# A planned attention and two feed-forward layers on one core: offsets on the planner's due times, one load for q and k, the last output in three pieces

## The chip, the core and the metric

The kernel runs on one core of a Trainium2 chip. The metric is the device time of one launch in microseconds (us). The engines are TensorE (PE in the profile, its weight loads PEld), VectorE (DVE), ScalarE (ACT), GpSimd (POOL) and SyncE (SP), which here issues every DMA.

## What is computed

Causal attention with a decay bias, 4 batches of 8 heads, 576 positions of 64 values; its output is seen as 2304 tokens of 512 values and goes through two feed-forward layers. Cut to what matters:

```python
scores = scale * np.matmul(q, k.transpose(0, 1, 3, 2))
bias = -(cum[:, :, :, None] - cum[:, :, None, :])
scores = np.where(causal, -1000000000.0, scores + np.minimum(bias, 0.0))
attn = np.exp(scores - scores.max(-1)); attn = attn / (attn.sum(-1) + 1e-09)
x = np.matmul(attn, v)                      # then as (2304, 512)
h = x @ w_in
x = (h * np.cos(h)) @ w_out                 # 512 -> 2048 -> 512
xn = x / np.sqrt(np.mean(x * x) + 1e-06) * rms_g
g = xn @ w_gate
out = (g / (1 + np.exp(-g)) * (xn @ w_val)) @ w_out2   # 512 -> 1536 -> 512
```

## The kernel before, in words

The Python program does not issue instructions as it goes. Each step is recorded with `plan.op(...)` (line 139): the engines that could run it with an estimated cost, the tiles it reads and writes, and a due time `plan.now + prio`. `Plan.order()` (line 156) then plays the whole program through a list scheduler with these estimated costs: an engine that is free takes, of the steps whose inputs are ready, the one with the smallest due time. The chip gets the result, one fixed list for each engine. On the chip an engine runs its list strictly in order and waits at each entry for its inputs, so a step that is late there holds up everything behind it on that engine. Two constants bend the choice: `HOLD` is added to the due time of an activation that needs another table than the one loaded, `KEEP_MODE` to a TensorE step of another array mode. Where a step has several engines, the one with the smallest estimated finish is taken, its own cost multiplied by `WEIGH` (line 133).

**Attention** goes over 16 pairs of heads. A pair loads q and k (lines 467 to 470, one transfer each into rings `qr` and `kr` of two buffers), its bias rows `ce` and `cp` (lines 473 to 476) and v. POOL writes the causal mask into the bias (line 491, line 484). TensorE makes scores (line 551; line 575 for the ragged last 64 positions), DVE adds the bias and takes the row minimum in one custom instruction (line 558, line 578; called "the bias step" below; its tile of minima is `mn`), ACT takes the exponential in place (line 586), TensorE transposes it (line 601), ACT or DVE copies the transpose from PSUM to `Pa` or `Pb` (line 336 on ACT, line 339 on DVE), TensorE multiplies by v (line 635), ACT or DVE copies to `xu`. Row sums are inverted (lines 513 and 515), go through DRAM (`rn_d`) and come back broadcast; DVE scales `xu` (line 347, the helper for all two-input steps) and the result is stored to `x_d`.

**Weights of the first layer** arrive as 64-bit integers' halves and are rebuilt by `value` (line 422): one step on POOL (line 430) or, as the other choice, on ACT (line 431), one on POOL (line 434), two on DVE (lines 435 and 437), then a split in two parts. 32 such chunks are done beside the attention.

**First layer (FF1).** Blocks of 256 or 512 tokens; each of 48 ticks does `gemm1` (line 734), cosine on ACT and DVE (`Sin` on line 852), a split, and `gemm2` (line 740). Its due times start at `T_FF1`, so its first ticks fill TensorE during the attention: tick k is due at `T_FF1 + k * P_FF1`, `gemm2` 1.6 `P_FF1` later, the weights' loads `LEAD_I` or `LEAD_O` earlier. Attention steps are due along `P_ATT` per pair. Transposed scores, scores and `gemm1` share the eight PSUM banks.

**Second layer (FF2)** multiplies on line 990 and line 1131 with seven products in place of eight block products. The last part (line 1131) goes over 9 units of 7 products `m`; a unit has two output tiles `o1` and `o2` of 128 rows by 512, stored whole at `m == 6` (lines 1154 to 1156).

The lines that say it shortest:

```python
o.alts, o.prio, o.table, o.dma = alts, self.now + prio, table, dma
t = max(ready, free[e] + ahead) + c * self.WEIGH[e]
_, _, o = min((o.prio + (self.HOLD if o.table and o.table != table else 0.0) + ..., o.seq, o)
              for o in avail[e] if o.ready <= t)
```

Of the kernel before, what the change touches and what calls it, by code (L numbers as in the profile page):

```python
# [44 lines left out]
P_ATT, P_FF1, P_SET, P_OUT = 6000.0, 8093.98, 7350.0, 2145.0  # L45
T_FF1 = 45000.0
# [235 lines left out]
def attention_moe_moe(ctx, tc, q2, k2, vp, s, w_in, w_out, w_gate, w_val, w_out2, rms_g, out):  # L282
# [120 lines left out]
    qr_r, kr_r = ring("qr", 2, [128, 640], F32, "att"), ring("kr", 2, [128, S], F32, "att")  # L403
# [18 lines left out]
    def value(src, after=()):  # L422
# [31 lines left out]
    class Run:  # L454


        def __init__(self, bp, parts):
            self.bp, self.b, self.p = bp, bp // NP, bp % NP
            self.qs = slice(0 if "a" in parts else 256, 640 if "b" in parts else 256)
            self.ks, self.vc = (S, 5) if "b" in parts else (256, 2)  # L460
            self.parts = {c: Part(self, c) for c in parts}
            self.col = {k: i for i, k in enumerate([(0, t) for t in range(4)] + ["p"] + [(1, t) for t in range(4)])}

        def load(self):
            bp, qn, ks = self.bp, self.qs.stop - self.qs.start, self.ks
            q, k = self.q, self.k = qr_r.new(), kr_r.new()
            load(lambda: q()[:, :qn], lambda: bass.AP(q2.tensor, q2.offset + bp * 128 * 640 + self.qs.start, [[640, 128], [1, qn]]), 512 * qn, [], [q], prio=0.0 if bp else -4.9e5)
            load(lambda: k()[:, :ks], lambda: bass.AP(k2.tensor, k2.offset + bp * 128 * S, [[S, 128], [1, ks]]), 512 * ks, [], [k], prio=0.0 if bp else -4.8e5)
# [10 lines left out]
        def masks(self, ts):  # L479
            c, cp = self.ce, self.cp  # L480
            for t in ts:
                if t == "p":
                    for e in range(2):
                        plan.op(on("POOL", 416, lambda e=e: pool.affine_select(
                            out=cp()[64 * e:64 * e + 64, 512:S], in_=cp()[64 * e:64 * e + 64, 512:S], pattern=[[-1, 64]], base=0, channel_multiplier=1,
                            compare_op=ALU.is_ge, fill=-8.0 * BIG)), [], [(cp, e)])
                else:
                    for e in range(2):
# [4 lines left out]
                            compare_op=ALU.is_ge, fill=-8.0 * BIG)), r, w)  # L493

        def load_v(self):
# [4 lines left out]
                 lambda: bass.AP(vp.tensor, vp.offset + self.bp * 128 * 640, [[640, 128], [1, 640]]), 327680, [], [vr])  # L500
# [9 lines left out]
        def factors(self):  # L510
# [3 lines left out]
                out=rs(), in0=rs(), scalar1=1e-9, scalar2=float(2.0 * np.pi), op0=ALU.add, op1=ALU.mult)), [], [rs])  # L514
            plan.op(on("DVE", 204, lambda: dve.reciprocal(out=rs(), in_=rs())), [], [rs])
            plan.op(on("PE", 109, lambda: pe.transpose(tr()[:9, :128], rs(), ident)), [rs], [tr], rows=0.1)
            copy(lambda: rt()[:9, :], lambda: tr()[:9, :128], 128, [tr], [rt], psum=True)
# [497 lines left out]
    n = 0  # L1015
# [194 lines left out]
```

## Time and profile before

| | us |
|---|---|
| median of 3 runs | 1005.22 |
| lowest and highest run | 1005.15, 1007.66 |
| the profiled execution | 1007.61 |
| its span, first to last instruction | 1005.6 |
| TensorE busy in that span | 986.7 |
| mean granted clock of TensorE | 0.996 of full speed |

The span is what the rows of the trace add up to; the profiled execution's own time stands 2.0 us above it and 2.4 us above the median. TensorE's busy time counts modelled ends of pipelined matmuls, so short waits between two matmuls can be hidden in it. A row of the view by stretches gives the stretch, its length, then busy us of PE, PEld, DVE, ACT and POOL with the number of instructions, the granted clock, the share of the DMA engines and GB/s. In rows of the timeline the bracket says how long the engine had stood idle and who released it.

### The profile page before, as it was taken

The page shows a single profiled execution, that of the slowest core. Times are in us where ns is not written, and L with a number is a line of the kernel's source. Part 1 is how long each engine was busy: PE and PEld are TensorE (multiplying, and loading weights), DVE is VectorE, ACT ScalarE, POOL GpSimd, SP SyncE. Part 2 cuts the span into 40 slices and gives each one's busy share as a digit, 9 for nine tenths or more (in the row PEclk, how much of TensorE's full clock was granted, in tenths as well). Part 3 has the DMA queues.
Part 4 walks back from the last instruction along what each step waited for, and adds up shares of the span by engine and source line. Part 5 has one row for each costly group of instructions (what it writes and reads, how often), then busy time and mean ns, then how long its engine had stood idle before and what let it go on. Part 6 is the DMA issues. An engine that isn't in the chain of part 4 may idle for free.

```text
span 1005.6 us, 17817 instructions
## 1 busy us (share of the span) xinstructions
PE 986.7 (98%) x5950; PEld 853.0 (85%) x5950; DVE 738.7 (73%) x1691; ACT 560.3 (56%) x1213; POOL 125.6 (12%) x252
## 2 busy tenths in 40 slices
PE   8899999999999999999999999999999999999998
PEld 5556776668988887877878999999999999999998
DVE  4688899885357799779766988865665678986661
ACT  6799998886456566557544765212211225575540
POOL 2444354520001101110110000000000000000000
PEclk9899999999999999999999999999999999999999
DMA  8899988966846774566644464827465477997761
GB/s 259 270 306 315 314 308 277 300 225 183 281 179 235 273 265 183 217 213 221 241 158 156 139 208 143 254 88 235 138 215 179 139 215 224 305 336 220 217 191 43
DMA packets 144237, 222.95 MB, mean 222 GB/s; under 512 B 13985, under 2 KB 98097, under 8 KB 144145
## 3 DMA queue, kind: packets, MB, share of 16 engines
q1 hardware_dynamic: 144144, 221.82, 67.5%
q8 instruction: 47, 0.77, 0.3%
q14 instruction: 46, 0.37, 0.1%
HBM read 146.71 MB, written 75.06 MB: 221 GB/s over the span
## 4 chain that ended last, share of the span: by engine, by line
PE 75%; DVE 11%; DMA 6%; issue 4%; ACT 2%; POOL 2%; SPq 0%; POOLq 0%; DVEq 0%; ACTq 0%
PE bank L990 25%; PE bank L734 15%; PE bank L740 14%; PE bank L1131 13%; DVE wk L347 3%; PE bank L635 2%; PE bank L601 2%; PE bank L551 2%; DVE wk L435 1%; DVE wg L347 1%; DVE wk L437 1%; DMA rn_d<-rt 1%; POOL wk L434 1%; DVE e L558 1%; DMA wk<-in_w_gate_dram 1%
## 5 line engine op out<-in xcount | busy, mean ns | idle before, releaser
L734 PE MATMUL bank<-xa,wi 128*128 128x256 f32 (+1 forms) x1152 | 216.7, 340 | 0.5 <-ACT Pb L336 0.5
L347 DVE TENSOR_TENSOR wk<-wk,bank 128x384 f32<-128x384 f32 (+2 forms) x237 | 130.6, 556 | 115.0 <-PE bank L990 39.2
L734 PEld LDWEIGHTS bank<-xa,wi 128*128 128x128 f32 x1152 | 180.1, 188 | 29.6 <-issue 1.9
L740 PE MATMUL bank<-wr,wg 128*128 128x512 f32 x672 | 165.8, 396 | 0.8 <-ACT wg L336 0.7
L740 PEld LDWEIGHTS bank<-wr,wg 128*128 128x128 f32 x672 | 125.1, 188 | 30.8 <-ACT wg L336 2.8
L990 PE MATMUL bank<-wr,wg 128*128 128x384 f32 x504 | 116.2, 338 | 0.0
L990 PE MATMUL bank<-wi,wg 128*128 128x384 f32 x504 | 115.4, 337 | 0.2 <-DVE t L347 0.2
L336 ACT ACTIVATE wg<-wk 128x512 fp32r<-128x512 f32 (+1 forms) x138 | 78.2, 579 | 48.5 <-DVE wk L347 33.8
L347 DVE TENSOR_TENSOR wg<-wk,wg 128x512 fp32r<-128x512 f32 (+1 forms) x148 | 89.4, 625 | 20.4 <-ACT wg L336 19.5
L434 POOL TENSOR_SCALAR wk<-wk 128x512 f32<-128x512 f32 x68 | 54.8, 809 | 327.8 <-ACT wk L431 307.8
L990 PEld LDWEIGHTS bank<-wr,wg 128*128 128x128 f32 x504 | 91.2, 188 | 0.0
L990 PEld LDWEIGHTS bank<-wi,wg 128*128 128x128 f32 x504 | 89.3, 188 | 1.2 <-DVE t L347 0.6
L850 ACT ACTIVATE wk<-bank,quarter 128x512 int32<-128x512 f32 x72 | 49.3, 684 | 55.1 <-PE bank L734 54.7
L586 ACT ACTIVATE e<-e,mn 128x128 f32<-128x128 f32 (+3 forms) x128 | 70.7, 555 | 9.4 <-DVE mn L558 9.0
L336 ACT ACTIVATE wr<-wr 128x384 fp32r<-128x384 f32 x108 | 55.8, 524 | 34.8 <-DMA wr<-g_S 15.0
L336 ACT ACTIVATE wk<-bank 128x512 f32<-128x512 f32 (+2 forms) x66 | 33.8, 531 | 73.8 <-PE bank L990 52.5
L852 ACT ACTIVATE wk<-wk,half_pi 128x512 f32<-128x512 f32 x72 | 52.1, 723 | 38.9 <-DVE wk L347 38.5
L1131 PE MATMUL bank<-wi,wr 128*128 128x256 f32 x585 | 73.7, 281 | 0.0
L347 DVE TENSOR_TENSOR wk<-bank,wk 128x512 f32<-128x512 f32 (+1 forms) x82 | 54.9, 669 | 23.4 <-ACT wk L852 23.3
L1131 PEld LDWEIGHTS bank<-wi,wr 128*128 128x128 f32 x585 | 71.2, 188 | 0.0
L435 DVE SCALAR_TENSOR_TENSOR wk<-wk 128x512 int32<-128x512 int32 x68 | 49.2, 725 | 21.2 <-POOL wk L434 21.2
L347 DVE TENSOR_TENSOR wr<-wr 128x384 fp32r<-128x384 f32 x108 | 56.6, 552 | 10.3 <-ACT wr L336 9.7
(126 smaller groups left out, 1547.5 us busy)
## 6 DMA issues: line engine op xcount, KB each, us to landing
wk<-in_w_out_dram SPq DMA_DIRECT2D x28, 512.0 KB, 4.7
wr<-g_S SPq DMA_DIRECT2D x54, 192.0 KB, 2.6
w_g<-wg SPq DMA_DIRECT2D x18, 512.0 KB, 3.4
w_v<-wg SPq DMA_DIRECT2D x18, 512.0 KB, 2.9
wr<-g SPq DMA_DIRECT2D x48, 192.0 KB, 3.5
g_S<-wk SPq DMA_DIRECT2D x45, 192.0 KB, 2.4
wk<-in_w_in_dram SPq DMA_DIRECT2D x16, 512.0 KB, 6.1
wo_d<-wg SPq DMA_DIRECT2D x16, 512.0 KB, 6.0
```

The costliest lines, as they stand in the source:

```text
L336: alts.append(("ACT", (act_p if psum else act_s)(n), lambda: act.activation(o(), i(), AF.Copy, scale=scale)))
L347: return plan.op(on("DVE", dve1(n), lambda: dve.tensor_tensor(out=o(), in0=a(), in1=b(), op=op)), r, w, **kw)
L434: plan.op(on("POOL", 660, lambda: pool.tensor_scalar(out=top().bitcast(F32), in0=top().bitcast(F32), scalar1=0.0, scalar2=1.0, op0=ALU.mul ...
L435: plan.op(on("DVE", 640, lambda: dve.scalar_tensor_tensor(out=top(), in0=low(), scalar=29, in1=top(), op0=ALU.logical_shift_right, op1=ALU ...
L551: pe.matmul(Sp[e]()[:, o:o + w], run.q()[hd, q0:q0 + 128], run.k()[hd, :w], start=True, stop=True)
L586: plan.op(on("ACT", act_s(w) + 187, lambda E=E, o=o, w=w, i=i, c=c: act.activation(E()[:, o:o + w], E()[:, o:o + w], AF.Exp, scale=-1.0, b ...
L734: pe.matmul(h, w[:, a, 128 * k:128 * k + 128], x[k // 2][:, k % 2, c, :blk], start=(n == 0), stop=(n == 11))
L740: pe.matmul(acc[t], g[a][:, 128 * t:128 * t + 128], w[:, c, :], start=(first and (a, c) == (0, 0)), stop=(last and (a, c) == (1, 0)))
L850: plan.op(on("ACT", act_p(512) + 93, lambda u=u, h=h: act.activation(u().bitcast(I32), h(), AF.Identity, bias=quarter)), [h], [u])
L852: plan.op(on("ACT", 628, lambda u=u: act.activation(u(), u(), AF.Sin, scale=-TWO_PI, bias=half_pi)), [], [u], table="sin")
L990: pe.matmul(bank_()[:, :HALF2], G[i]()[:, u, o + 128 * k:o + 128 * k + 128], xs[k]()[:, c, :], start=(first and n == 0), stop=(n == 5), sk ...
L1131: pe.matmul(bk_()[:, col:col + 256], gs[p // 3]()[:, u, 128 * (p % 3):128 * (p % 3) + 128], w3[p][i]()[:, c, o:o + 256], start=(n == 0), s ...
```

## The change

Three things. First, the planner's steps get an offset by kind, added to the due time (in ns, negative is earlier), and some constants change. Second, the host lays q and k side by side, 640 + 576 columns for each of a pair's 128 rows, and one transfer of 608 KB into one ring takes the place of two of 320 and 288 KB. Third, the last unit's output is stored in three pieces: the right half of `o2` after `m == 4`, `o1` after `m == 5`, the left half of `o2` after `m == 6`. The diff, cut to its core:

```diff
-LEAD_I, LEAD_O, LEAD_E = 14000.0, 10000.0, 0.0
+LEAD_I, LEAD_O, LEAD_E = 14000.0, 9847.0, 0.0
-KEEP_MODE = 1000.0
-DMA_EACH, DMA_RATE, DMA_LATE = 5.0, 21.6, 1700.0
+KEEP_MODE = 1306.0
+DMA_EACH, DMA_RATE, DMA_LATE = 5.0, 20.06, 1700.0
...
-P_ATT, P_FF1, P_SET, P_OUT = 6000.0, 8093.98, 7350.0, 2145.0
-T_FF1 = 45000.0
+P_ATT, P_FF1, P_SET, P_OUT = 6095.0, 8093.98, 7350.0, 2145.0
+T_FF1 = 47510.0
+O_LOAD, O_BIAS, O_V, O_MASK, O_SCORE, O_TTR, O_RAGGED = -1340.0, 2596.0, -218.0, -654.0, -1417.0, -2054.0, 310.0
+O_EXP, O_TR, O_P, O_PV, O_X, O_FACTOR, O_STORE = 2888.0, 96.0, -1290.0, -462.0, -4526.0, 114.0, 20.0
+O_VALUE, O_GEMM1, O_GEMM2, O_SIN, O_X1 = -1454.0, -2758.0, 2525.0, 916.0, 1195.0
...
-    WEIGH = {"PE": 1.0, "ACT": 1.0, "DVE": 2.0, "POOL": 1.0, "SP": 1.0}
-    SWITCH, HOLD = 1283.0, 30000.0
+    WEIGH = {"PE": 1.0, "ACT": 1.0, "DVE": 2.00, "POOL": 0.30, "SP": 1.0}
+    SWITCH, HOLD = 1283.0, 27846.0
...
-    qr_r, kr_r = ring("qr", 2, [128, 640], F32, "att"), ring("kr", 2, [128, S], F32, "att")
+    qk_r = ring("qk", 2, [128, 640 + S], F32, "att")
...
+            load(qk_t, lambda: qk[bp], 512 * (640 + S), [], [qk_t], run=4 * (640 + S), prio=O_LOAD if bp else -4.9e5)
...
-            for o, r0 in ((o1, 0), (o2, HALF2)) if m == 6 else ():
-                r0 += 2 * HALF2 * b + 128 * s3
-                load(lambda r0=r0: out[r0:r0 + 128, :], o, 1 << 18, [o], [])
+            r1 = 2 * HALF2 * b + 128 * s3
+            if unit < 3 * NB2 - 1:
+                parts = [(o1, 0, 0, 512), (o2, HALF2, 0, 512)] if m == 6 else []
+            else:
+                parts = {4: [(o2, HALF2, 256, 512)], 5: [(o1, 0, 0, 512)], 6: [(o2, HALF2, 0, 256)]}.get(m, [])
+            for o, r0, c0, c1 in parts:
+                load(lambda r0=r0 + r1, c0=c0, c1=c1: out[r0:r0 + 128, c0:c1], lambda o=o, c0=c0, c1=c1: o()[:, c0:c1], 512 * (c1 - c0),
+                     [o if c1 - c0 == 512 else (o, c0 // 256)], [], run=4 * (c1 - c0))
```

The offsets go to these steps: `O_LOAD` q and k, `O_BIAS` the loads of `ce` and `cp`, `O_V` v, `O_MASK` the masks, `O_SCORE` and `O_RAGGED` the scores, `O_TTR` the bias step, `O_EXP` the exponentials, `O_TR` the transposes, `O_P` the copies to `Pa` and `Pb`, `O_PV` the product with v, `O_X` its copy, `O_FACTOR` and `O_STORE` the row sums and the store, `O_VALUE` the four steps of `value`, `O_GEMM1`, `O_GEMM2`, `O_SIN` and `O_X1` FF1's parts. FF1's whole clock moves by `T_FF1`, 2510 ns later. No instruction of an engine is added or removed but for the DMAs named, and the split of line 430 against line 431.

## Rows read from the trace of the kernel before

**Rows 1.** The page's first part: busy time, share and instructions of each engine.

```profile
PE 986.7 (98%) x5950; PEld 853.0 (85%) x5950; DVE 738.7 (73%) x1691; ACT 560.3 (56%) x1213; POOL 125.6 (12%) x252
```

**Rows 2.** Stretches: length, then PE, PEld, DVE, ACT, POOL, clock, DMA, GB/s.

```profile
0.00:95.00 95.00, 86.60 (x591) 54.61 (x593) 68.65 (x238) 78.28 (x235) 37.53 (x109) 0.96 0.91 285
95.00:235.00 140.00, 134.84 (x938) 96.02 (x935) 119.71 (x317) 127.39 (x311) 58.69 (x108) 1.00 0.82 275
235.00:597.00 362.00, 361.17 (x1761) 300.36 (x1760) 273.86 (x563) 212.51 (x378) 29.34 (x36) 1.00 0.61 210
...
1002.30:1005.60 3.30, 0.00 (x0) 0.00 (x0) 0.40 (x1) 0.00 (x0) 0.00 (x0) 0.92 0.21 79
```

**Rows 3.** TensorE's waits up to 235 us: us in total, times, longest.

```profile
PE bank L601 <- ACT e L586: 4.0, 2, 3.2
PE bank L601 <- ACT Pb L336: 2.1, 3, 1.4
...
PE bank L575 <- ACT Pb L336: 1.3, 2, 1.0
PE bank L551 <- DVE mn L578: 1.2, 1, 1.2
PE bank L601 <- DVE mn L558: 1.1, 3, 0.6
PE bank L551 <- DVE mn L558: 0.6, 3, 0.2
PE bank L734 <- ACT Pb L336: 0.5, 1, 0.5
...
PE bank L575 <- ACT Pa L336: 0.3, 1, 0.3
```

**Rows 4.** The timeline between 33 and 41 us: start, us, engine, line, step.

```profile
33.91 1.78 PE L551 MATMUL bank<-kr,qr 64*128 64x128 f32 x12
...
36.51 0.54 POOL L491 TENSOR_SCALAR_AFFINE_SELECT ce<-ce 128x128 f32<-128x128 f32 x2 [2.97 <-DMA ce<-ce_d]
37.02 0.64 POOL L434 TENSOR_SCALAR wk<-wk 128x512 f32<-128x512 f32 x1
37.69 0.69 DVE L435 SCALAR_TENSOR_TENSOR wk<-wk 128x512 int32<-128x512 int32 x1 [3.61 <-POOL wk L434]
38.30 0.42 DVE L558 CUSTOM_DVE_ANT_0 e<-bank,ce 128x256 f32<-128x256 f32 x1
...
40.29 0.90 PE L601 MATMUL bank<-ident,e 128*128 128x128 f32 x3 [3.25 <-ACT e L586]
```

**Rows 5.** The stretch of the low clock, columns as in the view above.

```profile
39.10:46.00 6.90, 5.71 (x17) 3.02 (x19) 5.35 (x21) 5.57 (x21) 1.80 (x7) 0.51 0.94 286
```

**Rows 6.** Groups of ACT and of POOL up to 240 us: busy us, mean ns.

```profile
L430 POOL TENSOR_SCALAR wk<-wk 128x512 f32<-128x512 f32 x16 | 13.1, 818 | 20.2 <-DVE wg L347 13.1 <-DVE wi L347 6.2 <-issue 0.8
...
L431 ACT ACTIVATE wk<-wk 128x512 f32<-128x512 f32 x16 | 10.7, 677 | 2.5 <-DMA wk<-in_w_in_dram 1.4 <-DVE wg L347 1.0
```

**Rows 7.** SP's issues between 27 and 33 us.

```profile
27.33 0.53 SPq L351 DMA_DIRECT2D qr<-in_q_dram  x1
27.90 0.43 SPq L351 DMA_DIRECT2D kr<-in_k_dram  x1
28.44 1.03 SPq L351 DMA_DIRECT2D ce<-ce_d  x1
```

**Rows 8.** DMA issues by size: KB each, median us from issue to landing.

```profile
w_o<-wk SPq DMA_DIRECT2D x6, 256.0 KB, 2.0
...
w_o<-wk SPq DMA_DIRECT2D x6, 128.0 KB, 1.7
```

**Rows 9.** Line 430's instructions: ns min/median/max, first and last start.

```profile
L430 POOL TENSOR_SCALAR wk<-wk x16: 651/678/1165, 32.5 to 207.5; 128x512 f32<-128x512 f32 x16
```

**Rows 10.** Line 435's instructions, columns as for line 430.

```profile
L435 DVE SCALAR_TENSOR_TENSOR wk<-wk x68: 635/686/1127, 24.3 to 555.5; 128x512 int32<-128x512 int32 x68
```

**Rows 11.** The timeline of TensorE where its first FF1 matmul stands.

```profile
97.81 2.40 PE L734 MATMUL bank<-xa,wi 128*128 128x256 f32 x18 [0.48 <-ACT Pb L336]
```

More of the change, by code (lines that the diff above doesn't have):

```diff
@@ L464, in load @@
         def load(self):
[L465 to L468, printed above, removed]
+            bp, qk_t = self.bp, qk_r.new()
+            self.qk = qk_t
+            self.q, self.k = (lambda: qk_t()[:, :640]), (lambda: qk_t()[:, 640:])
+            load(qk_t, lambda: qk[bp], 512 * (640 + S), [], [qk_t], run=4 * (640 + S), prio=O_LOAD if bp else -4.9e5)
             c, cp = self.ce, self.cp = ce_r.new(), cp_r.new()
@@ L472, in load @@
                 load(lambda: c().rearrange("p e w -> p (e w)"), lambda: ce_d()[2 * bp:2 * bp + 2, :].rearrange("a b -> (a b)").partition_broadcast(128),
-                     1 << 19, [ce_d], [(c, (t, e)) for t in range(4) for e in range(2)])
+                     1 << 19, [ce_d], [(c, (t, e)) for t in range(4) for e in range(2)], prio=O_BIAS)
                 for e in range(2):
-                    load(lambda e=e: cp()[64 * e:64 * e + 64, :], lambda e=e: c_d()[2 * bp + e, :].partition_broadcast(64), 256 * S, [c_d], [(cp, e)], run=2304)
+                    load(lambda e=e: cp()[64 * e:64 * e + 64, :], lambda e=e: c_d()[2 * bp + e, :].partition_broadcast(64), 256 * S, [c_d], [(cp, e)], run=2304, prio=O_BIAS)
             else:
@@ L513, in factors @@
             plan.op(on("DVE", 130, lambda: dve.tensor_scalar(
[L514 to L517, printed above, removed]
-            load(lambda: dst().rearrange("a (b c) -> (a b) c", c=128), lambda: rt()[:9, :], 4608, [rt], [dst], run=512)
+                out=rs(), in0=rs(), scalar1=1e-9, scalar2=float(2.0 * np.pi), op0=ALU.add, op1=ALU.mult)), [], [rs], prio=O_FACTOR)
+            plan.op(on("DVE", 204, lambda: dve.reciprocal(out=rs(), in_=rs())), [], [rs], prio=O_FACTOR)
+            plan.op(on("PE", 109, lambda: pe.transpose(tr()[:9, :128], rs(), ident)), [rs], [tr], rows=0.1, prio=O_FACTOR)
+            copy(lambda: rt()[:9, :], lambda: tr()[:9, :128], 128, [tr], [rt], psum=True, prio=O_FACTOR)
+            load(lambda: dst().rearrange("a (b c) -> (a b) c", c=128), lambda: rt()[:9, :], 4608, [rt], [dst], run=512, prio=O_FACTOR)
             rb = self.rb = rb_r.new()
@@ L551, in qk @@
                         pe.matmul(Sp[e]()[:, o:o + w], run.q()[hd, q0:q0 + 128], run.k()[hd, :w], start=True, stop=True)
-            plan.op(on("PE", 110 + sum(1.668 * w for _, w in at.values()), qk), [run.q, run.k], Sp, mode=1)
+            plan.op(on("PE", 110 + sum(1.668 * w for _, w in at.values()), qk), [run.qk], Sp, mode=1, prio=O_SCORE)
             for t in reversed(ts):
@@ L601, in go @@
                     pe.transpose(tr()[:m, 128 * j:128 * j + 128], E[0]()[:, E[2] + c:E[2] + c + m], ident)
-            plan.op(on("PE", 109 * len(srcs), go), [(E[0], E[1]) for E in Es], [tr], rows=0.5)
+            plan.op(on("PE", 109 * len(srcs), go), [(E[0], E[1]) for E in Es], [tr], rows=0.5, prio=O_TR)
             cols = lambda n: tr()[:, :n].rearrange("p (c i) -> p c i", i=128)
             def out(o, src, n, P=P):
-                copy(o, src, n, [tr], [P], psum=True)
+                copy(o, src, n, [tr], [P], psum=True, prio=O_P)
             if i == 0:
@@ L644, in store @@
                 rb = self.run.rb
-                two(xu, xu, rb, S, [rb], [xu], op=ALU.mult)
-                load(lambda: xd()[:, p, :], xu, 512 * S, [xu], [(xd, p)])
+                two(xu, xu, rb, S, [rb], [xu], op=ALU.mult, prio=O_STORE)
+                load(lambda: xd()[:, p, :], xu, 512 * S, [xu], [(xd, p)], prio=O_STORE)
         def units(self):
@@ L851, in attention_moe_moe @@
             two(u, lambda u=u: u().bitcast(I32), h, 512, [h], [u], psum=True)
-            plan.op(on("ACT", 628, lambda u=u: act.activation(u(), u(), AF.Sin, scale=-TWO_PI, bias=half_pi)), [], [u], table="sin")
+            plan.op(on("ACT", 628, lambda u=u: act.activation(u(), u(), AF.Sin, scale=-TWO_PI, bias=half_pi)), [], [u], table="sin", prio=O_SIN)
             two(u, h, u, 512, [h], [u], op=ALU.mult, psum=True)
```

50 lines of the change are left out of this document (24 added, 26 removed).

## The prediction

> **What bounds the kernel now.** I read the page's busy line first [rows 1]. TensorE is busy for 986.7 of 1005.6 us, so all that any order can win by filling its idle time is 18.9 us, plus what waits hide inside "busy". The change takes no matmul away. The view by stretches says where the idle time lies [rows 2]: 8.4 us before 95 us (95 - 86.60), 5.2 us from 95 to 235 us (140 - 134.84), 0.8 us in the 362 us after that, and 3.3 us behind the last matmul. The last 770 us are a solid block of matmuls; only the attention stage and the tail can give anything. In the attention stage ACT is busy for 127.39 of 140 us and the DMA engines for 0.82 to 0.91 of the time [rows 2], so TensorE there stops for others. The table of its waits says for whom [rows 3]: for exponentials 4.0 us, for copies of the transposes to `Pb` and `Pa` 4.2 us (2.1 + 1.3 + 0.5 + 0.3), for the bias step 2.9 us (1.2 + 1.1 + 0.6).
>
> One wait stands out, of 3.25 us [rows 4]. The scores of line 551 end at 35.69 us, and the bias step of 256 columns on them stands at 38.30. DVE idled 3.61 us in between: its list has a weight step (line 435) ahead, which waits for POOL's weight step (line 434), and POOL's list has a mask ahead of that, which waits 2.97 us for the next pair's bias tile, landed at 36.51. So a late tile of the next pair stops this pair through two lists that are run in order; the exponential follows the bias step, and TensorE resumes at 40.29. Behind that stop the granted clock is 0.51 for 6.9 us [rows 5]: the lower of the two levels, 1.2 GHz. The mean of 0.96 before 95 us [rows 2] is this one dip (6.9 x 0.49 / 95 = 0.036); the rest is at 2.4.
>
> About 0.3% (3.0 us) is what a measurement of this kernel can tell from no change: "same" means 1002.2 to 1008.2.
>
> **The sum.** It is made against the profiled execution's own 1007.61 us, which is 2.4 us above the median.
>
> *Bias step ahead of weight work.* `O_TTR` moves it 2054 ns earlier; the weight steps move 2510 - 1454 = 1056 ns later with FF1's clock. That is 3.1 us of preference, so the step at 37.69 should leave its place ahead of line 558: 38.30 - 35.69 = 2.6 us [rows 4]. What is late next is the bias tile itself: it still lands at 36.51, and the next pair's first bias step needs it; I give 1.0 us back for that. Then the clock: the dip's 5.71 busy us [rows 5] would take half at full clock, so 2.85 us. The other waits of rows 3 are at most 1.4 us, and the clock stayed up behind them; a stop of about 1 us is nearer to those than to 3.25, so I count the dip as gone. Term -4.4; ends 0 and -6.1 (the whole 3.25 and the dip). Of the 2.9 us of other waits for the bias step [rows 3] I take a third, -1.0; ends 0 and -2.9.
>
> *Copies ahead of exponentials, work off ACT.* `O_P` (-1290) and `O_EXP` (+2888) put a copy 4.2 us ahead of an exponential that was due with it. POOL's weight of 0.30 turns its estimate for the first step of `value` from 700 into 210 ns against ACT's 575, so most of the 16 steps that ACT still does move: up to 16 x 0.677 = 10.7 us off ACT [rows 6], the engine with 9% idle. Half of the 4.2 us of waits for copies goes: -2.1; ends 0 and -4.2. The price is on the other side: the exponentials' own waits (4.0 us, of them 3.2 in the stop above [rows 3, 4]) can return elsewhere. +1.0; ends 0 and +4.0, those waits doubled.
>
> *q and k in one transfer.* SP's issues of a pair, 0.53 and 0.43 us [rows 7], become one, and the bias load queued behind them goes out some 0.5 us earlier. The same bytes go through the same engines, so the landing of k does not move, and the score, which needs both, waits as before. What hides it: q and k of the pair go out at 27.33 us, and its first score is in the matmuls from 33.91 us on [rows 4, 7], 6.6 us later. Term 0; ends -0.5 (the bias tile 0.5 us earlier in the stop) and +0.5, a late score once.
>
> *Bias loads later.* `O_BIAS` is +2596, but the weights' loads move by 2510 to 2663 too, so only q, k and v gain on `ce`, and q and k were ahead of it already [rows 7]. SP's list is in order: behind a late `ce` stand the weights' load and the store of `xu`, and POOL's mask waits for it. +0.7; ends 0 and +2.6, the whole offset once.
>
> *FF1's `gemm2` later.* With T_FF1 `gemm2` is due 5.0 us later and `gemm1` 0.2 earlier, so it has more slack for its weights, at most the 0.8 us idle after 235 us [rows 2]. -0.4; ends 0.8 either way.
>
> *The tail.* After the last matmul come one DVE step, a store and the end, 3.3 us [rows 2]. The last store shrinks from 256 to 128 KB; transfers of these sizes land in 2.0 and 1.7 us [rows 8]. -0.3; ends 0 and -0.6. The two earlier pieces are issued while matmuls run; if they landed late they would still end before the last.
>
> `HOLD` falls by 2.2 us of 30 while the exponentials move 2.9 and `Sin` 3.4 us (2510 + 916) later, so tables change about as often; one change more would lie in the 12.6 us that ACT idles between 95 and 235 us (140 - 127.39) [rows 2] and, if that cover is gone, in the waits for copies already counted. `KEEP_MODE` and the rest (`O_X`, `O_PV`, masks) change order within the same waits: 0, with the ends above.
>
> Sum: -4.4 - 1.0 - 2.1 + 1.0 + 0 + 0.7 - 0.4 - 0.3 = -6.5. That is 1001.1 for the profiled execution, and 1005.22 - 6.5 = **998.7 us** for the median. With all ends good it is -15.1 (990.1), with all bad +7.9 (1013.1).
>
> **The rivals.**
>
> *All waits go.* The planner weighs all steps together, and PEld's idle inside "busy" may shrink as well. Then the good ends of the first terms hold: -6.1 - 2.9 - 4.2, with the last three as above -13.2, so 992.0. For: the stops are few and each has a named cause. Against: the DMA engines at 0.91 before 95 us [rows 2] set when bias tiles land. 10%.
>
> *The waits move.* The chip's times are not the planner's, and each list is run in order, so a stop that is taken out comes back at the next late tile. Only 2.6 - 1.0 us of the stop and the tail's 0.3 remain, and the dip stays: 1003.3. The offsets then do not do what they say. For: ACT at 91% of 95 to 235 us and DVE at 86% [rows 2] leave little to rearrange. 17%.
>
> *POOL and DVE block each other.* The step on line 430 takes 651 ns at best and 818 on average, 1165 at worst [rows 6, 9]; line 435 on DVE runs from 635 to 1127 [rows 10]. If each moved step costs DVE a worst case, that is 16 x 0.49 = 7.9 us on an engine with 20.3 us idle between 95 and 235 us [rows 2]; half of it reaches TensorE, 4.0, so 1002.7. Against: line 434 waits elsewhere on its inputs, and the median of both lines is near the minimum. 8%. By the Trainium skill (SBUF — State Buffer, Who interferes with whom), a DVE instruction with two SBUF inputs contends with a GpSimd instruction that reads SBUF, and the later one is blocked fully; the spread of the rows named agrees with that, and by that rule alone the sum would be -2.5.
>
> *Slower: the bias tile of an early pair lands later.* The place is POOL's wait of 2.97 us for `ce` [rows 4]. Up to 97.81 us there is no FF1 matmul to fill in [rows 11], and the DMA engines are 0.91 busy. If `O_BIAS` lets v or a weights' load pass, a stop grows by 2.6 us and keeps its dip of 2.85: 5.4 us a pair. One such pair only eats the other gains; from two on it decides: +10.9, less 2.8 from the other terms (-1.0 - 2.1 + 1.0 - 0.4 - 0.3), gives 1013.3. Against: `ce` waits for its buffer of two pairs before, so its issue follows that release and hardly the due time. 10%.
>
> **How the numbers follow.** The forecast has 55% and lies between 995 and 1002.2. With the first rival that makes 0.65 for faster, the second and third 0.25 for the same, the last 0.10 for slower. The range is 993.0 to 1005.5: it holds the forecast and both rivals near 1003 with some room for the bad ends, and leaves out the slower rival and the far half of the first.
>
> **What would show it.** Right: no weight step that waits for POOL ahead of line 558; no dip of the clock between 30 and 50 us, mean clock 1.00 before 95 us; TensorE's idle time before 235 us at 8 to 10 us in place of 13.6; line 430 more often than 16 times up to 240 us and ACT under 85% busy between 95 and 235 us; one `qk` issue a pair; the last store landing 0.3 us sooner. Wrong: two dips, POOL's waits for `ce` longer than 3 us, or idle time after 235 us that was not there. The forecast fails as a whole if TensorE's waits for ACT and DVE stay at 11 us under other names.

## The result, and the profile after

| | before | after |
|---|---|---|
| median, us | 1005.18 (1000.93 to 1007.66, 4 runs) | 989.91 (989.80 to 990.68, 4 runs) |
| ratio, 95% interval | | 0.9854 [0.982, 0.9888] |
| profiled execution, its span, us | 1007.61, 1005.6 | 990.68, 988.8 |

The change takes 15.3 us off (1005.18 - 989.91), more than twice the 6.5 forecast, and lands 3.1 us below the range. Line numbers of the new kernel are higher: by one from the scores to the exponentials (552, 559, 587, 602, 735), by three in the helpers and in `value` (339, 350, 433, 434, 437, 438).

The busy line of the page of the kernel after answers to [rows 1]:

```profile
PE 979.8 (99%) x5950; PEld 853.2 (86%) x5950; DVE 733.4 (74%) x1671; ACT 548.6 (55%) x1215; POOL 137.7 (14%) x266
```

The span fell by 16.8 us (1005.6 - 988.8). TensorE runs the same 5950 matmuls and is busy 6.9 us less (986.7 - 979.8); its idle time fell from 18.9 to 9.0 us (988.8 - 979.8), which is the other 9.9. The view by stretches of the kernel after, columns as in [rows 2], says where:

```profile
0.00:95.00 95.00, 90.59 (x654) 60.06 (x656) 69.73 (x241) 81.85 (x260) 40.79 (x117) 1.00 0.90 299
95.00:235.00 140.00, 138.58 (x967) 102.14 (x962) 123.04 (x310) 124.32 (x310) 65.51 (x113) 1.00 0.87 284
235.00:597.00 362.00, 362.00 (x1754) 303.11 (x1754) 273.08 (x570) 209.72 (x373) 31.45 (x36) 1.00 0.60 213
...
985.60:988.80 3.20, 0.05 (x1) 0.00 (x0) 0.42 (x1) 0.00 (x0) 0.00 (x0) 0.90 0.12 41
```

Idle time before 95 us is 4.4 us where it was 8.4, from 95 to 235 us 1.4 where it was 5.2. From there to the tail it is nothing, where it was 2.0 (0.8 up to 597 us and 1.2 from 597 to 868). So 7.7 of the 9.9 us of idle time were won in the attention stage. Read the counts too: up to 235 us TensorE has issued 1621 matmuls (654 + 967) against 1529 (591 + 938). What most of those 92 are stands in the view by source line of FF1's `gemm1` up to 235 us (ns min/median/max, first and last start), of the kernel before:

```profile
L734 PE MATMUL bank<-xa,wi x216: 274/281/497, 97.8 to 232.5; 128*128 128x256 f32 x108
```

and of the kernel after:

```profile
L735 PE MATMUL bank<-xa,wi x288: 274/282/496, 90.9 to 233.8; 128*128 128x256 f32 x144
```

72 more matmuls of `gemm1` are done by 235 us, and 18 more of `gemm2` (95 before, 113 after). In busy time that is 8.8 us (30.1 before, 38.9 after) and 3.9 us (25.9 and 29.8), together 12.7 us of work which the block behind no longer has to do. That is how a gain in this stage shows: not as an earlier end of one stop, but as FF1 work pulled forward into it. With the 2.0 us of idle time behind 235 us and 0.2 of the tail it makes 14.9 of the 16.8 us by which the span fell; in the other 1.9 the same matmuls behind 235 us are busy for less time, and no wait names the reason.

TensorE's waits up to 235 us in the kernel after, answering to [rows 3]:

```profile
PE bank L722 <- POOL ident masks.py:199: 1.5, 1, 1.5
PE bank L552 <- DVE mn L559: 0.8, 1, 0.8
PE bank L602 <- ACT Pb L339: 0.7, 2, 0.4
PE bank L576 <- DVE mn L559: 0.6, 1, 0.6
PE bank L636 <- DVE mn L559: 0.6, 2, 0.4
PE bank L552 <- ACT Pb L339: 0.5, 1, 0.5
...
PE bank L552 <- DVE mn L579: 0.2, 1, 0.2
```

The 4.0 us for exponentials are gone altogether, copies of the transposes fell from 4.2 to 1.2 (0.7 + 0.5), the bias step from 2.9 to 2.2 (0.8 + 0.6 + 0.6 + 0.2).

"Busy" fell by 6.9 us with the same matmuls. The dip of the clock is 2.85 of them [rows 5]; with it the transposes went from 50.5 to 48.0 us and the ragged scores from 22.4 to 20.7. The other 4 us are not traced. Less waiting hidden inside "busy" does not show: in the kernel before the weight loads of line 601 stood idle for 15.9 us behind exponentials and copies to `Pb` (7.4 + 8.5), TensorE itself for 6.1 of them (4.0 + 2.1); in the kernel after it is 10.3 (3.6 + 6.7) and 0.7. The part that only the weight loads show is 9.8 and 9.6 us.

At the place of the stop [rows 4] the timeline of the kernel after reads:

```profile
32.57 0.54 POOL L492 TENSOR_SCALAR_AFFINE_SELECT ce<-ce 128x128 f32<-128x128 f32 x2 [2.34 <-DMA ce<-ce_d]
32.63 0.42 DVE L559 CUSTOM_DVE_ANT_0 e<-bank,ce 128x256 f32<-128x256 f32 x1 [1.71 <-PE bank L552]
...
33.75 0.78 DVE L350 TENSOR_TENSOR wi<-wk,wi 128x512 fp32r<-128x512 f32 x1
...
34.65 0.65 POOL L433 TENSOR_SCALAR wk<-wk 128x512 f32<-128x512 f32 x1
```

The bias tile is late here too (2.34 us, before 2.97), but the bias step waits for its scores and for nothing else. The late tile holds up the step that needs it, no longer two lists.

### The profile page after: what moved, and what is told of

Same layout as the page of the kernel before. It is cut to its first block, busy times and chain, and to the rows that moved or that the text cites. A ratio compares the mean times of both kernels' runs of the same rounds, so it can differ in the third digit from the quotient of the medians.

```text
span 988.8 us, 17827 instructions
## 1 busy us (share of the span) xinstructions
PE 979.8 (99%) x5950; PEld 853.2 (86%) x5950; DVE 733.4 (74%) x1671; ACT 548.6 (55%) x1215; POOL 137.7 (14%) x266
## 4 chain that ended last, share of the span: by engine, by line
PE 90%; ACT 3%; DMA 3%; issue 2%; DVE 2%; POOL 0%; SPq 0%; POOLq 0%; DVEq 0%; ACTq 0%
PE bank L991 27%; PE bank L735 20%; PE bank L741 19%; PE bank L1132 14%; PE bank L636 3%; PE bank L602 3%; PE bank L552 2%; ACT e L587 1%; PE bank L576 1%; PE bank L822 1%; ACT Pb L339 1%; DMA ce<-ce_d 1%; DMA wk<-in_w_in_dram 1%; DMA cp<-c_d 1%; DMA rn_d<-rt 0%
## 5 line engine op out<-in xcount | busy, mean ns | idle before, releaser
L350 DVE TENSOR_TENSOR wg<-wk,wg 128x512 fp32r<-128x512 f32 (+1 forms) x148 | 91.7, 639 | 17.5 <-ACT wg L339 17.3
L339 ACT ACTIVATE wg<-wk 128x512 fp32r<-128x512 f32 (+1 forms) x133 | 74.7, 577 | 45.8 <-DVE wk L350 33.5
L587 ACT ACTIVATE e<-e,mn 128x512 f32<-128x512 f32 (+3 forms) x128 | 70.8, 561 | 4.0 <-DVE mn L559 3.9
L339 ACT ACTIVATE wr<-wr 128x384 fp32r<-128x384 f32 x108 | 55.1, 524 | 31.6 <-DMA wr<-g_S 17.1
L350 DVE TENSOR_TENSOR t<-t,bank 128x384 f32<-128x384 f32 x72 | 39.8, 553 | 31.3 <-PE bank L991 28.9
```

What stands on the lines that cost most here:

```text
L339: alts.append(("ACT", (act_p if psum else act_s)(n), lambda: act.activation(o(), i(), AF.Copy, scale=scale)))
L350: return plan.op(on("DVE", dve1(n), lambda: dve.tensor_tensor(out=o(), in0=a(), in1=b(), op=op)), r, w, **kw)
L587: plan.op(on("ACT", act_s(w) + 187, lambda E=E, o=o, w=w, i=i, c=c: act.activation(E()[:, o:o + w], E()[:, o:o + w], AF.Exp, scale=-1.0, b ...
```

## The experiments

The order of this kernel is made by a planner, so an edit has two kinds of effect: what it does itself, and that the whole list is drawn anew. Runs that edit the finished list, and pairs that differ in one constant, are there to tell these apart. The kernel before scatters by some 10 us from run to run, and each batch of runs had its own runs of it, with medians of 1005.2 to 1006.5; ratios are against those.

### Is the one stop worth what its wait shows?

One entry of DVE's finished list, the weight step that stood at 37.69 us, goes behind the four bias steps that it held up:

```diff
     order = plan.order()
+    dv = [i for i, o in enumerate(order) if o.eng == "DVE"]
+    ln = [order[i].fn.__code__.co_firstlineno for i in dv]
+    j = next(j for j in range(len(dv)) if ln[j:j + 7] == [435, 437, 435, 558, 558, 558, 558])
+    order.insert(dv[j + 6], order.pop(dv[j + 2]))
```

> The kernel before, one entry of DVE's list moved: the weight step of line 435 that waited for POOL at 37.7 us goes behind the four bias steps that follow it; all other lists are as they were. Theory 'named causes' (few stops with a cause each carry the gain): the stop of 3.25 us shrinks to about 1, the clock does not dip, 4 to 6 us faster than before, 999 to 1001. Rival 'waits move' (the next pair's late bias tile stops TensorE instead): the dip stays, under 1.7 us faster, 1003.5 or more.

Measured: 1007.24 us (1003.24 to 1009.66, 10 runs), ratio 1.0011 [0.9991, 1.0031]: nothing gained. This is the rival's 1003.5 or more. The timeline of this kernel:

```profile
34.99 0.42 DVE L558 CUSTOM_DVE_ANT_0 e<-bank,ce 128x256 f32<-128x256 f32 x1 [1.15 <-PE bank L551]
...
45.31 0.94 POOL L491 TENSOR_SCALAR_AFFINE_SELECT ce<-ce 128x128 f32<-128x128 f32 x2 [0.67 <-DMA ce<-ce_d]
...
46.23 1.91 POOL L434 TENSOR_SCALAR wk<-wk 128x512 f32<-128x512 f32 x2
...
46.92 0.69 DVE L435 SCALAR_TENSOR_TENSOR wk<-wk 128x512 int32<-128x512 int32 x1 [1.06 <-POOL wk L434]
...
47.53 0.42 DVE L558 CUSTOM_DVE_ANT_0 e<-bank,ce 128x256 f32<-128x256 f32 x1
...
49.52 0.55 PE L601 MATMUL bank<-ident,e 128*128 128x128 f32 x3 [1.58 <-ACT e L586]
```

The stop at 35 us is gone: line 558 follows its scores. Twelve us later the same chain stands again: late `ce`, mask, POOL's weight step, DVE's weight step, bias step, exponential, and TensorE idle for 1.58 us. The late tile is only part of that stop: POOL waited 0.67 us for it, and DVE 1.06 us for POOL. Later in the same execution come stops that the kernel before did not have there: TensorE waits 2.12 us for the bias step of line 578 at 119.10 us, and the granted clock is 0.87 from 120 to 130 us and 0.86 from 170 to 180, where it was 1.00 from 100 to 200 us before. So the length of a wait in the trace was not what its removal gave; other stops of the in-order lists took it back. This is the rival "the waits move", true for a single edit of the old list.

### Does taking weight steps off ACT pay?

In the lists of after, 14 of POOL's 30 first weight steps go back to ACT, each in its place; in the lists of before, 14 of ACT's 16 go to POOL (engine and function of the finished entry are exchanged):

```diff
+    moved = [o for o in order if o.eng == "POOL" and len(o.alts) == 2][::2][:14]
+    for o in moved:
+        o.eng, _, o.fn = o.alts[1]
...
```

> The changed kernel with its lists unchanged but for 14 of the 30 first weight steps that POOL took, which go back to ACT at the same place of the order (16 and 16 as before). Theory 'named causes': 14 x 0.68 = 9.5 us more on ACT, of which about half reaches TensorE: 3 to 6 us slower than the changed kernel, 993 to 996. Rival 'hidden': ACT has room at those places, within 1.5 us of 989.9.

> The kernel before with its lists as they are, but for 14 of the 16 first weight steps that ACT had, which go to POOL at the same place of the order. Theory 'work off ACT', as a price that holds in any order: 3 to 6 us below before. Rival 'waits move': POOL's list, in order, puts its masks behind these steps, which wait for weights; within 2 us of before or slower.

Measured: 995.36 us (994.40 to 997.83, 4 runs), 5.5 us slower than after by the medians and 4.0 by the ratios (0.9894 against 0.9854, whose intervals overlap); and 1005.66 (10 runs), ratio 1.0009 [0.9989, 1.0028], nothing. So in the old lists less work on ACT is worth nothing. In the new ones it looks like a gain, but a random disturbance of the offsets lost as much (next experiment), and `a_act` cannot tell the two apart. The groups of line 433 and 434 up to 240 us in the kernel after, answering to [rows 6]:

```profile
L433 POOL TENSOR_SCALAR wk<-wk 128x512 f32<-128x512 f32 x30 | 25.1, 837 | 22.1 <-DVE wg L350 11.2 <-DVE wi L350 7.7 <-DMA wk<-in_w_in_dram 1.4
...
L434 ACT ACTIVATE wk<-wk 128x512 f32<-128x512 f32 x2 | 1.4, 722 | 0.0
```

30 steps where there were 16, at 837 ns on average where it was 818.

### How much do the offsets carry?

The kernel after with its 19 offsets at zero, and with each moved at random by up to 200 ns:

```diff
-O_LOAD, O_BIAS, O_V, O_MASK, O_SCORE, O_TTR, O_RAGGED = -1340.0, 2596.0, -218.0, -654.0, -1417.0, -2054.0, 310.0
+O_LOAD, O_BIAS, O_V, O_MASK, O_SCORE, O_TTR, O_RAGGED = 0.0, 0.0, 0.0, 0.0, 0.0, 0.0, 0.0
...
```

> The changed kernel planned anew with all 19 offsets at 0; constants, POOL's weight, the one load for q and k and the three stores stay. Theory 'named causes': the offsets carry most of the gain, so 998 to 1003. Rival 'constants': P_ATT, T_FF1 and POOL's weight carry it, 993 or less.

> The changed kernel planned anew with each of the 19 offsets moved at random by up to 200 ns either way; every rule (bias step ahead of weights, copies ahead of exponentials) stays in force. Theory 'named causes': the rules carry it, so within 2 us of 989.9. Rival 'picked order': the gain belongs to the very lists that were picked, and a neighbour loses 4 us or more, 994 or above.

Measured: 992.36 us (991.88 to 999.13, 4 runs) without offsets, 995.18 (993.52 to 997.03) with disturbed ones. Both went against the theory and with the rival. So 12.8 of the 15.3 us come without any offset, and offsets close to those chosen did no better than none (ratios 0.9896 and 0.9883, one random draw). With the new constants they show no rule on which step should go first; they look like a pick of one good list among its neighbours, worth about 2.5 us. What they would give on the old constants was not run.

### Which part carries the rest?

From the kernel before upward: one load for q and k with the three stores; the same with POOL's weight at 0.30; and after with offsets zero and POOL's weight 1.0, which is the first with all new constants.

```diff
-    WEIGH = {"PE": 1.0, "ACT": 1.0, "DVE": 2.00, "POOL": 0.30, "SP": 1.0}
+    WEIGH = {"PE": 1.0, "ACT": 1.0, "DVE": 2.00, "POOL": 1.0, "SP": 1.0}
```

> The kernel before, planned anew with q and k in one transfer and the last output in three pieces; all offsets 0, old constants, POOL's weight 1.0. Theory 'work off ACT' (POOL's weight carries most of what the offsets don't): q and k are hidden, so 1004 to 1007, as before. Rival 'one transfer' (SP's list and the DMA engines get free earlier, all tiles land sooner): 1000 or less. Rival 'any new plan is as good as another draw': anywhere from 993 to 1007.

> The run with q and k in one transfer and three stores, and POOL's weight 0.30; offsets 0, old constants. Theory 'work off ACT': some 10 us less on ACT, half of it for TensorE, so 5 to 8 us below that run. Rival 'constants' (P_ATT, T_FF1 and the DMA rate carry it): within 2 us of that run.

> The changed kernel planned anew with all offsets 0 and POOL's weight back at 1.0; new constants, one transfer, three stores. Theory 'work off ACT': it loses 5 us or more against the run with offsets at 0 (992.4), 997 to 1003. Rival 'constants': 994 or less.

Measured: 1003.22 us (ratio 0.9977 [0.9957, 0.9998], 10 runs), 1003.54 (0.9972 [0.995, 0.9994], 10 runs), 995.38 (0.9909 [0.988, 0.9938], 4 runs). POOL's weight gives nothing here, against the theory, and `b_const` came out between its forecasts. The constants are the large step: from `b_qk` to `b_const` 7.8 us by the medians, 6.8 by the ratios, whose intervals do not meet. They were then put into `b_qk`, the base from here on (the kernel before with one transfer and three stores), by thirds, and the transfer rate alone was taken out of `b_const`:

```diff
 c_rate:
-DMA_EACH, DMA_RATE, DMA_LATE = 5.0, 21.6, 1700.0
+DMA_EACH, DMA_RATE, DMA_LATE = 5.0, 20.06, 1700.0
 c_tff1:
-T_FF1 = 45000.0
+T_FF1 = 47510.0
 c_mode:
-KEEP_MODE = 1000.0
+KEEP_MODE = 1306.0
...
 c_norate:
-DMA_EACH, DMA_RATE, DMA_LATE = 5.0, 20.06, 1700.0
+DMA_EACH, DMA_RATE, DMA_LATE = 5.0, 21.6, 1700.0
```

(`c_tff1` has the new `LEAD_O` as well, `c_mode` the new `HOLD` and `P_ATT`.)

> The run with one transfer and three stores (offsets 0, POOL's weight 1.0, old constants: 1003.2), planned anew with DMA_RATE 20.06 in place of 21.6 alone: the planner takes transfers to be slower. Theory 'rate' (a planner that expects tiles too early queues steps behind late tiles; the right rate takes the stops out): 995 to 998, close to the run with all new constants (995.4). Rival 'FF1's clock' (T_FF1 alone gives the attention its lead): 1002 to 1005.

> The same base, with FF1's clock alone: T_FF1 47510 and LEAD_O 9847. Theory 'FF1's clock' (weights' loads and steps 2.5 us later let bias tiles and the attention's chain pass): 995 to 998. Rival 'rate': 1002 to 1005.

> The same base, with KEEP_MODE 1306, HOLD 27846 and P_ATT 6095 alone. Both theories: 1001 to 1005, no gain. If it comes to 998 or less, neither 'rate' nor 'FF1's clock' is the cause but the changes of mode or table.

> The run with offsets 0, POOL's weight 1.0 and all new constants (995.4), but DMA_RATE back at 21.6. Theory 'rate': 1000 or more. Rival 'FF1's clock': 994 to 997.

| kernel | median, us (range, runs) | ratio to before, 95% |
|---|---|---|
| rate alone | 996.65 (995.75 to 1005.48, 10) | 0.9939 [0.9908, 0.9969] |
| `T_FF1`, `LEAD_O` alone | 1000.09 (998.24 to 1006.94, 10) | 0.9958 [0.9929, 0.9987] |
| `KEEP_MODE`, `HOLD`, `P_ATT` alone | 1001.69 (1000.58 to 1006.36, 10) | 0.9975 [0.9954, 0.9996] |
| all constants but the rate | 1000.58 (997.48 to 1006.55, 10) | 0.9948 [0.9919, 0.9977] |

The rate is the largest single part: 6.6 us by the medians when put in (1003.22 - 996.65), 5.2 when taken out (1000.58 - 995.38). By the ratios, into which two runs at 1005 us weigh, it is 3.8 and 3.9 us. The other two thirds give 3.1 and 1.5 us by the medians, too little to tell from a new draw of the list; the intervals of the rate and of `T_FF1` overlap. `T_FF1` came out between its two forecasts.

### The rate, or a lucky list?

The rate is a constant of the planner alone; the chip does not see it. The planner charges a row of 4096 bytes 5 + 4096 / rate ns on each of 16 engines: 194.6 ns at 21.6, or 337 GB/s in all; 209.2 ns and 313 GB/s at 20.06; 361 GB/s at 23.2; 291 at 18.6. What the chip delivers when the transfers fill the engines shows in the view by stretches of the kernel before (the last two columns):

```profile
50.00:75.00 25.00, 24.01 (x178) 14.94 (x174) 22.33 (x77) 23.35 (x74) 11.32 (x28) 1.00 0.96 308
75.00:100.00 25.00, 23.11 (x171) 14.99 (x170) 21.20 (x72) 23.63 (x73) 11.66 (x29) 1.00 0.99 317
100.00:125.00 25.00, 24.99 (x188) 18.44 (x187) 20.03 (x53) 24.24 (x54) 9.30 (x18) 1.00 0.97 309
```

308 to 317 GB/s at a share of 0.96 to 0.99 looks like the new rate. But these are rows of all sizes, and 337 and 313 GB/s are the rates for rows of 4096 bytes alone. Row by row the trace says something else. Up to 235 us its packets took 201.3 us on an engine (0.91 x 95 + 0.82 x 140 [rows 2]); the planner's formula for the same packets gives 197.0 at 21.6 and 211.6 at 20.06. The 8320 rows of 4096 bytes there took 192.5 ns on average, against 194.6 and 209.2. So over the stage the old constant is 2% too fast and the new one 5% too slow; in the full stretch from 50 to 125 us (72.9 us on an engine against 70.3 and 75.5) they are equally far off. By the Trainium skill (Perfetto Trace Analysis, Roofline) a core's share of HBM is 358 GB/s, and one core alone can pull more; by that figure the old constant was not too fast, and the rows of 4096 bytes agree. As far as the packets tell, the new rate is a margin that the planner leaves for transfers, not a match with the chip.

To test it, the same random offsets were put on the base without and with the new rate, the rate was taken out of after, and it was moved the wrong way at both ends (23.2 on the base, 18.6 on after). The last run has rate and POOL's weight together, the pair of `b_pool`.

```diff
-DMA_EACH, DMA_RATE, DMA_LATE = 5.0, 21.6, 1700.0
+DMA_EACH, DMA_RATE, DMA_LATE = 5.0, 23.2, 1700.0
```

> The base run (one transfer, three stores, all else old: 1003.2) with the 19 offsets drawn at random within 200 ns of 0: how far a neighbouring plan with the old rate lies. Theory 'rate': 1001 to 1006, still in the old group. Rival 'draws' (the constants only draw another plan): it can as well come to 996.

> The same random offsets with DMA_RATE 20.06, all else as the base. Theory 'rate': 4 to 7 us below its pair with the old rate, 994 to 999. Rival 'draws': no order between the two.

> The whole change but for DMA_RATE, which is back at 21.6. Theory 'rate': it loses 4 to 6 us, 994 to 996 or more. Rival 'offsets cover it': within 2 us of 989.9.

> The base run with DMA_RATE 23.2, the same step in the other direction: the planner takes transfers to be faster still. Theory 'rate': slower than the base, 1005 or more. Rival 'draws': anywhere between 995 and 1006.

> The whole change with DMA_RATE 18.6, a further step of the same kind: the planner takes transfers to be slower than the chip shows them in its fullest stretches (some 19.4 bytes per ns and DMA engine). Theory 'right rate' (the gain comes from matching the chip): no further gain, 990 to 995. Rival 'the slower the better' (any margin against late tiles pays): 988 or less, faster than the change.

> The kernel before with one transfer, three stores, DMA_RATE 20.06 and POOL's weight 0.30; offsets 0, all other constants old. Theory 'off ACT pays once the stops are gone' (POOL's weight gave 0 with the old rate, 3 with the new constants): 2 to 4 us below the run with the rate alone (996.65), 992.5 to 994.5. Rival 'POOL's weight never pays by itself': 996 or more.

| kernel | median, us (range, runs) | ratio to before, 95% |
|---|---|---|
| base, random offsets, rate 21.6 | 1001.18 (997.33 to 1004.86, 7) | 0.9947 [0.9919, 0.9975] |
| the same offsets, rate 20.06 | 996.25 (994.05 to 1004.30, 9) | 0.9912 [0.9881, 0.9943] |
| base, rate 23.2 | 1009.86 (1007.24 to 1016.47, 10) | 1.005 [1.002, 1.0079] |
| after, rate 21.6 | 993.96 (992.75 to 995.26, 4) | 0.987 [0.9843, 0.9897] |
| after, rate 18.6 | 997.42 (996.54 to 999.57, 5) | 0.9911 [0.9879, 0.9943] |
| base, rate 20.06, POOL 0.30 | 995.75 (995.06 to 996.03, 4) | 0.9895 [0.9863, 0.9927] |

Five pairs differ in the rate alone. Waits and idle time are those up to 235 us of each profiled execution (`b_qk`, `b_pool` and `c_rate` have there the slow start of the last section):

| from rate 21.6 to 20.06 | medians, us | fastest runs, us | POOL's waits for bias tiles, us | TensorE idle, us |
|---|---|---|---|---|
| `b_qk` to `c_rate` | -6.57 | -2.83 | 21.7 to 11.0 | 11.0 to 8.9 |
| `b_qk_jit` to `c_rate_jit` | -4.93 | -3.28 | 24.0 to 13.8 | 9.3 to 8.4 |
| `b_pool` to `c_rate_pool` | -7.79 | -3.88 | 24.7 to 14.0 | 11.2 to 8.4 |
| `c_norate` to `b_const` | -5.20 | -3.35 | 29.6 to 15.3 | 10.1 to 7.9 |
| `a_norate` to after | -4.05 | -2.95 | 34.3 to 29.2 | 7.3 to 5.8 |

All five go the same way in every column, and on the base the times are in the order of the rates: 1009.86, 1003.22, 996.65. The ratios' intervals are apart in the third pair and overlap in the others; rate 23.2 stands apart from both others. By the fastest runs, which a slow start is unlikely to have touched, the rate is worth some 3 us. A rate of 18.6 gave 997.42 us where 990 to 995 was expected. But within the whole change the rate cannot be told from leaving the picked list: `a_norate` loses 4.1 us (1.6 by the ratios) and `a_slow` 7.5, offsets moved at random 5.3. With the rate in, POOL's weight comes out between its forecasts: 0.9 us by the medians, 4.4 by the ratios.

The waits show where the rate acts. POOL and DVE up to 235 us in the pair with the same offsets, at 21.6:

```profile
POOL ce L492 <- DMA ce<-ce_d: 13.8, 8, 3.8
...
POOL cp L485 <- DMA cp<-c_d: 10.2, 9, 2.8
DVE wk L438 <- POOL wk L437: 7.5, 6, 2.3
```

and at 20.06:

```profile
POOL ce L492 <- DMA ce<-ce_d: 11.0, 9, 2.8
DVE wk L438 <- POOL wk L437: 4.0, 4, 2.3
POOL cp L485 <- DMA cp<-c_d: 2.8, 6, 1.1
```

POOL stands less often at a mask whose bias tile is not there yet; with the rate at 23.2 it is 51.6 us (31.6 + 20.0). DVE's waits for weight steps behind POOL fall in the first three pairs and stay in the last two (9.7 to 9.4, 5.3 to 5.5). That a planner which counts transfers longer puts such steps later in its lists fits this; the lists themselves were not compared.

From before to after the waits change in another way. The kernel before:

```profile
POOL ce L491 <- DMA ce<-ce_d: 19.9, 12, 3.7
...
POOL cp L484 <- DMA cp<-c_d: 15.2, 14, 4.2
...
DVE wk L435 <- POOL wk L434: 14.1, 10, 3.6
...
DVE e L558 <- POOL ce L491: 1.5, 2, 1.0
```

and the kernel after:

```profile
POOL ce L492 <- DMA ce<-ce_d: 22.8, 8, 4.7
...
POOL cp L485 <- DMA cp<-c_d: 6.4, 8, 1.7
...
DVE e L559 <- POOL ce L492: 7.3, 5, 4.4
DVE wk L438 <- POOL wk L437: 5.5, 7, 1.6
```

POOL's waits fell from 35.1 to 29.2 us. DVE waited 14.1 us for weight steps that stood behind a waiting mask and 1.5 for the masks; after, 5.5 and 7.3. The bias step waits longer for its own tile, and the weight work is less caught behind it. This is not the rate's doing: `a_norate`, with the old rate, has 5.3 us for weight steps and 5.1 for the masks.

The stretches of the pair with the same offsets show what TensorE has of the rate, first at 21.6:

```profile
0.00:95.00 95.00, 87.89 (x598) 55.00 (x599) 70.63 (x238) 78.97 (x243) 43.68 (x109) 0.98 0.90 296
95.00:235.00 140.00, 137.82 (x964) 100.36 (x965) 119.54 (x331) 130.28 (x313) 57.23 (x107) 1.00 0.86 277
```

and at 20.06:

```profile
0.00:95.00 95.00, 90.94 (x650) 58.88 (x652) 75.42 (x255) 84.08 (x255) 42.98 (x115) 1.00 0.93 303
95.00:235.00 140.00, 135.66 (x945) 99.25 (x942) 123.54 (x328) 127.91 (x303) 48.52 (x92) 1.00 0.85 281
```

Idle time before 95 us falls from 7.1 to 4.1 us, the clock does not dip, and 52 more matmuls are out. From 95 to 235 us part of it is lost again: idle time grows from 2.2 to 4.3 us, and 33 matmuls of the lead are left.

## Why the prediction was wrong

The direction was right (faster, 0.65), and so was the stage. The nearest case was the first rival, "all waits go", 992.0 at 10%; with the good ends of all terms the sum was 990.1. The range stopped at 993.0.

**The step that failed** is "`KEEP_MODE` and the rest (`O_X`, `O_PV`, masks) change order within the same waits: 0". `DMA_RATE` and `P_ATT`, which stand in the same diff, got no term, `HOLD` had 0 too, and `T_FF1` entered only as a shift beside the offsets. What the runs show in place of that 0 is 3.8 to 6.6 us for the rate alone (`b_qk` to `c_rate`) and 6.8 to 7.8 for all constants together (`b_qk` to `b_const`). I argued from the offsets, where the diff is longest. From kernel to kernel along the ladder:

| step | by medians, us | by ratios (x 1005.2), us |
|---|---|---|
| one load for q and k, three stores | -2.8 | -2.3 |
| the rate | -6.6 | -3.8 |
| the other constants | -1.3 | -3.0 |
| POOL's weight 0.30 | -3.0 | -2.6 |
| the 19 offsets | -2.5 | -2.9 |

(The first column starts at 1006.06, before's median beside `b_qk`.) By either column the constants and the weight carry 9.4 to 10.9 us, the offsets under 3. That holds for this order of the steps, with the offsets last. Of the forecast's -6.5 all but the tail came from terms that rest on offsets, with POOL's weight or `T_FF1` beside them. The rate alone does not explain the miss: the whole change without it (`a_norate`) stands at 993.96 us, 4.7 under the forecast of 998.7, and the rate takes off the other 4.1.

The second failure is in the sizes. By the waits in the two profiles the large terms came out better than forecast: 6.1 us for the stop and its dip where 4.4 stood, 3.0 for copies where 2.1 stood, and none of the prices of 1.0, 1.0 and 0.7. All terms read that way make 11.6 us (6.1 + 0.7 + 3.0 + 0.8 + 0.8 + 0.2; the first 0.8 are exponentials outside the stop) where 6.5 stood. The argument against "all waits go" was that the DMA engines set when bias tiles land. POOL still waits 29.2 us for them, but less stands behind it.

**Bias step ahead of weight work, -4.4.** The place was right: no weight step stands before line 559 there, and the clock's mean before 95 us is 1.00. But the place alone is not the gain: the stop taken out by itself gains nothing (`b_moved`), because stops return elsewhere, which I had put at 1.0. In the list after, both the 3.25 us and the dip are gone. The dip is also not in every execution: of the 98 executions of the kernel before that stand beside the runs above, 44 have a mean granted clock of 0.999 or 1.000, where such a dip alone takes off 0.003, and a median of 1004.4 us; the other 54 have a lower clock and 1007.5. The forecast took the dip's whole 2.85 us off a median. Other waits for the bias step: -0.7 (2.9 to 2.2), forecast -1.0.

**Copies ahead of exponentials, work off ACT, -2.1 + 1.0.** TensorE's waits for copies fell by 3.0 us; those for exponentials did not return, they went from 4.0 us (3.2 of them the stop) to none, so the +1.0 had the wrong sign. POOL took 14 of ACT's 16 steps, as forecast. "ACT under 85% busy" was wrong: 124.32 of 140 us is 89%, because the relief was filled. Up to 235 us ACT is busy for 206.17 us (81.85 + 124.32), before 205.67 (78.28 + 127.39): it makes 148 copies to `Pa` and `Pb` in place of 119, for DVE only 12 in place of 41, and more of FF1. The exponentials are 144 both times.

**q and k in one transfer, 0.** The view of DMA issues of the kernel after has one a pair (KB each, median us to landing):

```profile
qk<-in_qk_dram SPq DMA_DIRECT2D x16, 608.0 KB, 7.4
```

With the stores it measured -2.3 to -2.8 us, outside my ends. Whether the transfer itself or the new list does that is not settled; the stores' own part is small (below).

**Bias loads later, +0.7.** Right in kind, nothing in time: POOL's waits for `ce` grew from 19.9 to 22.8 us and the bias step waits 7.3 us for masks, but TensorE waits for the bias step no more than before and has FF1's work from 90.9 us on. One sign of being wrong came true without harm: POOL's longest wait for `ce` is 4.7 us, over the 3 that I named. **`gemm2`, -0.4:** the 0.8 us idle after 235 us is gone, the good end. **The tail, -0.3:** the last DVE step starts 3.33 us ahead of the end of the span before and 3.11 after (988.8 - 985.69): -0.2. **`HOLD`:** table changes up to 240 us fell from 17 to 13 (lines 852 and 586, after 853 and 587), not "about as often"; what that is worth was not separated.

**The rivals.** "POOL and DVE block each other" did not come. 14 more steps on POOL cost the kernel before nothing (`b_poolfix`), and taking them off POOL in the kernel after costs 5.5 us (`a_act`); line 438 on DVE ran at 632/693/1153 ns (least, median, most), line 435 before at 635/686/1127. The rule of the Trainium skill cited there (SBUF — State Buffer, Who interferes with whom) may hold for the single step, as these spreads allow, but no run here shows a loss from it. "The waits move" is true of one edit and false of the change. The slower rival, a bias tile that stops a pair for 5.4 us, did not come: TensorE's longest wait after the start is 0.8 us.

Open: why a rate slower than the trace's rows makes better lists; what of the first step's 2.8 us is the transfer; the shares of `T_FF1`, `KEEP_MODE`, `HOLD` and `P_ATT`; the offsets on the old constants; the rate within the final list. No version tried beat the kernel after.

## What to carry to other kernels

Where a planner makes the order, give each of its constants a term in the forecast, also those that the chip does not see: here one number, a transfer rate set 7% lower, was worth 3 to 7 us, as much as 19 tuned offsets or more. Compare such a constant with the trace row by row and not with the GB/s of a busy stretch; and if it pays, do not conclude that it matches the chip. Do not price a stop of an in-order list by its length: take it out alone before you count on it, since other stops can stand behind it. Offsets found by search belong to one list; the one small disturbance tried lost what they gave, so they are set last.

## What was not expected of the hardware

In some executions the first matmuls run at half their pace for far longer than in others. TensorE's timeline of the profiled execution with the new rate alone (1004.90 us, of a kernel whose fastest eight runs end by 998.90):

```profile
6.05 3.78 PE L704 MATMUL bank<-ep,eight 32*128 32x512 f32 x4
9.76 3.36 PE L552 MATMUL bank<-qk 64*128 64x512 f32 x8
...
17.24 1.91 PE L602 MATMUL bank<-ident,e 128*128 128x128 f32 x8
```

and of `b_const` (994.13 us), where the same matmuls come in the same order:

```profile
6.05 2.18 PE L704 MATMUL bank<-ep,eight 32*128 32x512 f32 x4
8.16 1.77 PE L552 MATMUL bank<-qk 64*128 64x512 f32 x8
...
12.06 1.04 PE L602 MATMUL bank<-ident,e 128*128 128x128 f32 x8
```

3.78 us against 2.18 and 3.36 against 1.77, at the same start of 6.05 us. That looks like the lower of the clock's two levels, 1.2 GHz against 2.4: in the dip of the kernel before, at a granted clock of 0.51, four matmuls of line 551 took 1.65 us, and 0.92 soon after it. The slow pace lasts to about 21 us, and the next load of q and k is issued at 20.80 in place of 14.02 us, so some 7 us are lost. The granted clock of the view by stretches reads 1.00 there in both, so the level is inferred from the matmuls' durations alone. The profiles of `a_zero` (999.13 us, its other runs near 992), `b_qk` and `b_pool` start in the same way. That this is also what sets the other run of the rate alone at 1005 us is likely and was not seen; what makes one execution start slow is open. By the Trainium skill (TensorE: Matmul & The Clock Gate, Part 1: The HAM clock gate) the number of slow matmuls at the start varies from run to run and the loss stays under 1% of a typical span; the profiles agree with the first, and 7 us of 1003, 0.7%, with the second.
